# A recurrence on 128-row units: w, k, r channel-major, whole-row scans, matmuls on quarters of the array, fp32 combine

## The chip, the cores and the metric

The kernel runs on one core of a Trainium2 chip. The metric is the device time of one execution in microseconds (us). The engines of the core are named as in the profile: PE (TensorE; its weight loads are PEld), DVE (VectorE), ACT (ScalarE), POOL (GpSimd), and SP, whose queue issues the DMAs.

## The reference

A recurrence with a decaying state per head, and behind it a soft mixture of experts over all tokens. B = 4 batches, H = 8 heads, S = 768 tokens, D = 48 channels; the mixture has 3072 tokens of 384 values, 8 experts with 4 slots each, and 1024 hidden values. All is float32.

```python
state = zeros(B, H, D, D)
for t in range(S):
    cur = einsum('bhd,bhe->bhde', u[None] * kt, vt)
    y[:, :, t] = einsum('bhd,bhde->bhe', rt, state + cur)
    state = wt[:, :, :, None] * state + einsum('bhd,bhe->bhde', kt, vt)
x = y.transpose(0, 2, 1, 3).reshape(B * S, H * D)
logits = x @ phi                                  # 3072 x 32
d = softmax(logits, axis=0);  slot_input = d.T @ x
slot_out[e] = relu(slot_input[e] @ w1[e]) @ w2[e]   # 8 experts x 4 slots
c = softmax(logits, axis=1);  out = c @ slot_out
```

## The kernel before, in words

The work is cut into 16 **pairs**: one batch and two heads (head h on rows 64h to 64h+47 of a 112-row tile). A pair has six **chunks** of 128 tokens. Inside a chunk the decay is taken out by cumulative products: K is divided by the product up to a token and R multiplied by it, so that the chunk becomes a masked score matrix; between chunks a 48x48 state is carried.

For each pair w, k and r come from memory with tokens on the rows (L173). PE transposes w (`a_wT`, L200) and k and r (`a_turn`, L235). DVE makes the backward products G, one scan of 128 per chunk (`a_back`, L212), the forward products Rc from their reciprocals (`a_fwd`, L221), and the scaled KTt and RTt (`a_scale`, L241). PE then turns KTt back (`b_kn`, L279), makes the scores (`b_scores`, L292), the chunk states U (`b_u`, L313) and the two parts of y: masked scores times v (`c_av`, L335) and R times the carried state (`c_inter`, L348). DVE carries the state by a scan per head over U (`b_state`, L321) and adds the diagonal part when it moves y out of PSUM (`c_evac`, L357). That diagonal part is r times k times u, summed: two products on POOL (`d_rk` L254, `d_rku` L260), a sum on DVE (`d_a`, L265), a product with v on POOL (`d_av`, L270). POOL also masks the scores (L297). Then x is transposed (L366) and multiplied with phi (L383), and each batch adds its slot inputs (L428).

The order of each engine's instructions is written out by hand in a loop over 17 steps. A step issues part A (scans and scaling) of one pair, parts B and C (scores, state, y) of the pair before, and the transposes of x for the one before that. Nothing reorders them: an instruction that waits holds back all that stands behind it on its engine. Weights of the experts arrive through the same SP queue during the loop and at its end.

The tail is the experts: `up_proj` (L515), `down_proj` (L549) in two groups of output columns (240 and 144), and `mix` (L593), which combines the slots per token. `mix` splits both factors into a high and a low part in fp32r and contracts 128 rows in one pass; 24 token tiles for each group of columns. The output leaves in 14 stores.

## Time and profile before

| what | value |
|---|---|
| time, median of 3 runs | 245.69 us (244.47 to 246.1) |
| profiled execution, span | 244.0 us |
| PE busy | 211.9 us (87%) |
| DVE busy | 183.7 us (75%) |
| POOL busy | 106.6 us (44%) |
| ACT busy | 97.2 us (40%) |
| mean granted PE clock | 0.946 |
| moved by DMA | 49.54 MB, mean 203 GB/s |

Busy times are shares of the span in which an engine works on an instruction; several engines are busy at once, so they do not add up. The granted clock is the share of PE's full clock that the chip allowed, here in stretches of 3.41 us. The first scan starts at 5.12 us, the first matmul of `up_proj` at 199.93 us; what follows, to the end of the span, is called the tail below.

### The profile page before, as it was taken

The numbers are of one execution on the slowest core, as the hardware profiler recorded it, in microseconds if no ns is written. First come the engines' busy times: TensorE is split into PE (matmuls) and PEld (weight loads), VectorE is DVE, ScalarE is ACT, GpSimd is POOL, SyncE is SP. The second block draws the span as 40 slices with busy tenths as digits, with TensorE's granted clock in tenths as the row PEclk, the third lists the DMA queues.
The fourth block names the chain that finished last, engine by engine and source line by source line (L and its number), as shares of the span: only waits on it lengthen the run. The fifth ranks groups of instructions, "written<-read, shape, count | busy, mean of one in ns | idle before, by whom it ended". The sixth has DMA issues, their size and how long they took to land.

```text
span 244.0 us, 7186 instructions
## 1 busy us (share of the span) xinstructions
PE 211.9 (87%) x2824; PEld 158.8 (65%) x2824; DVE 183.7 (75%) x464; ACT 97.2 (40%) x265; POOL 106.6 (44%) x156
## 2 busy tenths in 40 slices
PE   7759798989898899989798989897989999979850
PEld 3448586868677667768596768687768652346650
DVE  4997969798989888899979798999793744203540
ACT  0623436445262616372544354353536531203330
POOL 5346478465472828382737274563725131000000
PEclk9997979999997999999979999997999999999975
DMA  4988958939795969698696959994959278994994
GB/s 93 181 171 150 178 104 180 199 107 185 223 225 156 230 164 271 119 249 162 207 173 206 179 185 180 309 233 185 288 177 313 68 248 273 318 326 145 334 309 120
DMA packets 122072, 49.54 MB, mean 203 GB/s; under 512 B 101424, under 2 KB 118960, under 8 KB 122032
## 3 DMA queue, kind: packets, MB, share of 16 engines
q1 hardware_dynamic: 122032, 49.02, 79.2%
q8 instruction: 24, 0.39, 0.7%
q14 instruction: 16, 0.13, 0.2%
HBM read 44.29 MB, written 4.72 MB: 201 GB/s over the span
## 4 chain that ended last, share of the span: by engine, by line
PE 44%; DVE 38%; issue 6%; DMA 5%; SPq 2%; ACT 1%; POOL 1%; DVEq 0%; POOLq 0%; ACTq 0%
DVE Rc L221 13%; PE yp L348 13%; DVE G L212 12%; PE yp L335 6%; DVE Sb L321 6%; DVE KTt L241 5%; DMA wt<-in_moe_w_dram 4%; PE wt L200 4%; PE tp L279 4%; PE so L549 3%; PE hp L515 3%; PE op L593 3%; SPq L173 2%; PE sp L428 2%; PE tp L235 2%
## 5 line engine op out<-in xcount | busy, mean ns | idle before, releaser
L270 POOL TENSOR_TENSOR av<-vt,a 128x576 f32<-128x576 f32 x16 | 18.6, 1162 | 60.0 <-DVE x L357 38.9
L235 PE MATMUL tp<-ident,wrk 128*112 128x128 f32 x192 | 32.1, 299 | 13.8 <-DVE KTt L241 13.1
L212 DVE TENSOR_TENSOR_SCAN G<-wt,floor 112x128 f32<-112x128 f32 x96 | 32.0, 401 | 9.9 <-PE wt L200 9.6
L221 DVE TENSOR_TENSOR_SCAN Rc<-wt,Rc,ceil 112x127 f32<-112x127 f32 x96 | 37.6, 459 | 0.6
L348 PE MATMUL yp<-Sb,RTt 112*64 112x96 f32 x320 | 33.7, 353 | 3.8 <-DVE Sb L321 3.3
L235 PEld LDWEIGHTS tp<-ident,wrk 128*112 128x112 f32 x192 | 20.6, 140 | 24.2 <-DVE KTt L241 17.7
L297 POOL TENSOR_SCALAR_AFFINE_SELECT at<-at 128x384 f32<-128x384 f32 x64 | 31.8, 520 | 10.3 <-ACT at L296 10.2
L296 ACT COPY at<-ap 128x384 f32<-128x384 f32 x64 | 27.6, 482 | 20.6 <-PE ap L292 19.8
L281 ACT COPY kn<-tp 128x336 f32<-128x336 f32 (+1 forms) x32 | 11.0, 397 | 56.2 <-PE tp L279 56.2
L335 PEld LDWEIGHTS yp<-vt,at 128*64 128x64 f32 x768 | 29.0, 150 | 3.9 <-issue 1.6
L292 PE MATMUL ap<-RTt,KTt 48*128 48x128 f32 x384 | 30.9, 289 | 0.0
L335 PE MATMUL yp<-vt,at 128*64 128x48 f32 x768 | 30.8, 234 | 0.0
L292 PEld LDWEIGHTS ap<-RTt,KTt 48*128 48x128 f32 x384 | 24.8, 187 | 5.7 <-issue 4.7
L348 PEld LDWEIGHTS yp<-Sb,RTt 112*64 112x64 f32 x320 | 22.3, 157 | 7.2 <-DVE Sb L321 6.1
L254 POOL TENSOR_TENSOR rk<-wrk 128x576 f32<-128x576 f32 x16 | 22.6, 1414 | 9.4 <-ACT rk L205 8.7
L321 DVE TENSOR_TENSOR_SCAN Sb<-up,pat 48x288 f32<-48x288 f32 x32 | 24.0, 749 | 2.1 <-PE up L313 1.9
L260 POOL TENSOR_TENSOR rk<-rk,u_bc 128x576 f32<-128x576 f32 x16 | 22.5, 1405 | 1.9 <-DMA u_bc<-in_u_dram 1.7
L357 DVE TENSOR_TENSOR x<-yp,av 128x288 f32<-128x288 f32 x32 | 14.5, 454 | 7.8 <-PE yp L348 7.7
L241 DVE TENSOR_TENSOR RTt<-tp,Rc 112x384 f32<-112x384 f32 x32 | 16.5, 553 | 2.2 <-PE tp L235 1.8
L241 DVE TENSOR_TENSOR KTt<-tp,G 112x384 f32<-112x384 f32 x32 | 16.0, 538 | 0.0
L200 PE MATMUL wt<-ident,wrk 128*112 128x128 f32 x96 | 14.0, 282 | 1.3 <-POOL rk L254 0.7
L205 ACT ACTIVATE rk<-wrk,b_low 128x576 f32<-128x576 f32 x16 | 12.6, 786 | 6.5 <-DVE a L265 6.5
(125 smaller groups left out, 280.0 us busy)
## 6 DMA issues: line engine op xcount, KB each, us to landing
wt<-in_moe_w_dram SPq DMA_DIRECT2D x24, 512.0 KB, 4.9
wt<-in_moe_w_dram SPq DMA_DIRECT2D x4, 1536.0 KB, 6.9
vt<-in_v_dram SPq DMA_DIRECT2D x16, 288.0 KB, 4.0
wrk<-in_w_dram SPq DMA_DIRECT2D x30, 144.0 KB, 2.9
wrk<-in_k_dram SPq DMA_DIRECT2D x30, 144.0 KB, 3.4
wrk<-in_r_dram SPq DMA_DIRECT2D x30, 144.0 KB, 3.9
wt<-in_moe_w_dram SPq DMA_DIRECT2D x5, 576.0 KB, 8.2
wt<-in_moe_w_dram SPq DMA_DIRECT2D x3, 960.0 KB, 8.5
```

Of the source, the lines that this page charges most:

```text
L200: nc.tensor.transpose(out=wt[0:PITCH, c // 3, (c % 3) * P:(c % 3 + 1) * P], in_=win(st["t"], W_OFF, c), identity=ident)
L212: nc.vector.tensor_tensor_scan(out=G[0:PITCH, c, 0:P][:, ::-1], data0=wc[:, ::-1], data1=floor[0:PITCH].broadcast_to([PITCH, P]), initial= ...
L221: nc.vector.tensor_tensor_scan(out=Rc[0:PITCH, c, 1:P], data0=wc[:, 0:P - 1], data1=ceil[0:PITCH].broadcast_to([PITCH, P - 1]), initial=Rc ...
L235: nc.tensor.transpose(out=tp[0:PITCH, j, :], in_=win(st["t"], off, 3 * hf + j), identity=ident)
L241: nc.vector.tensor_tensor(out=st[which][0:PITCH, cs, :], in0=st[which, hf][0:PITCH], in1=fac[0:PITCH, cs, :], op=ALU.mult)
L254: nc.gpsimd.tensor_tensor(out=rk, in0=chd(st["t"], R_OFF), in1=chd(st["t"], K_OFF), op=ALU.mult)
L292: nc.tensor.matmul(out=aps[h][:, cc, :], lhsT=st["KT"][rows, c, :], rhs=st["RT"][rows, c, :], start=True, stop=True)
L296: nc.scalar.copy(out=at, in_=aps[h])
L297: nc.gpsimd.affine_select(out=at, in_=at, pattern=[[0, 3], [1, P]], compare_op=ALU.is_gt, fill=0.0, base=0, channel_multiplier=-1)
L321: nc.vector.tensor_tensor_scan(out=Sb[rows, h * D:(h + 1) * D, :].rearrange("p e n -> p (e n)"), data0=st["up"][rows].rearrange("p e n -> ...
L335: nc.tensor.matmul(out=yp[cols, cc, h, :], lhsT=st["AT", h, hf][:, cc, cols], rhs=st["vv"][:, h, 3 * hf + cc, :], start=first[th], stop=False)
L348: nc.tensor.matmul(out=st["yp", hf][cols, cc], lhsT=st["RT"][0:PITCH, c, cols], rhs=Sb[0:PITCH, :, c], start=False, stop=(cc == 2))
```

## The change

The host now delivers w, k and r **channel-major** (channels on rows, 768 tokens along a row, with one extra column per chunk: 6 x 129 = 774), and rearranges the output. The rows of a tile are filled: a **unit** has 128 rows, heads 2g and 2g+1 on 48 rows each, and on the 16 rows left over beside each a third of heads 6 and 7. So three units hold a batch's eight heads, and the fourth pair of the batch (heads 6 and 7) is put together from the three scaled units by DMAs from SBUF to SBUF (`a_gather`).

For a unit DVE runs one backward scan over 774 elements (`a_back`, L505; a column of 3e38 restarts it at each chunk), one reciprocal, one product for k in place (`a_k`, L512), one forward scan (`a_fwd`, L515), one product for r in place (`a_r`, L520). No transposes of w, k, r are left on PE. The diagonal part is one product on POOL per unit (`a_rk`, L501, 768 columns), and PE sums it against u into four columns per chunk (`aP`, L572), in the same PSUM bank as U; a DVE copy takes it out (L585). `b_kn` (L535), `b_scores` (L548), `c_inter` (L616) and the transposes of x (`l_turn`, L647) each work on quarters of the array: 64 rows by 64 columns, four places. `b_state` is one scan of 288 for both heads (L588), followed by an ACT copy to a contiguous Tc (L595). All PSUM tiles are fixed; U, aP and the turned k share one bank, y has one buffer for each head.

In the tail there are three groups of columns (160, 160, 64). The slots are gathered onto all four 32-row groups by one matmul (`gather_slots`, L229), and `mix` (L242) is a plain fp32 product of 32 rows, all token tiles of one row group before the next. Output leaves in 5 stores. The later expert weights go into the buffers that the loop frees.

On DVE, one step of the loop for an ordinary pair of **before** (G and Rc are the products of the next pair, Sb the state, x the evacuation):

```order
L304 MEMSET up 128x48
L212 SCALAR_TENSOR_TENSOR G<-wt,floor 112x128 x6
L215 RECIPROCAL Rc<-G 112x6
L221 SCALAR_TENSOR_TENSOR Rc<-wt,Rc,ceil 112x127 x6
L241 TENSOR_TENSOR KTt<-tp,G 112x384 x2
L321 SCALAR_TENSOR_TENSOR Sb<-up,pat_142 48x288 x2
L241 TENSOR_TENSOR RTt<-tp,Rc 112x384 x2
```

There the clearing of U (up) stands ahead of the scans. On DVE in **after**, the third step of a batch and the start of the fourth (blkw holds w, krb k and r of a unit, tp_80 U and aP, Traw the state):

```order
L505 SCALAR_TENSOR_TENSOR G<-blkw,G 128x774
L507 RECIPROCAL blkw<-G 128x6
L512 TENSOR_TENSOR krb_94<-krb_94,G 128x774
L515 SCALAR_TENSOR_TENSOR G<-blkw,G 128x774
L565 MEMSET tp_80 128x48
L588 SCALAR_TENSOR_TENSOR Traw<-tp_80,blkm 112x288
L585 COPY asb_110<-tp_80 128x24
L636 TENSOR_TENSOR x_100<-y_82,av_105 128x6x48
L636 TENSOR_TENSOR x_100<-y_83,av_105 128x6x48
L84 TENSOR_REDUCE nM<-lt 96x1
L520 TENSOR_TENSOR krb_94<-krb_94,G 128x774
```

The clearing of U (L565) has moved behind the scans and products of the step, and the state scan stands right behind it. On PE in **after**, one step from the matmuls that wait for that clearing to the next such place:

```order
L572 MATMUL tp_80<-cst,blka 64x4 x12
L578 MATMUL tp_80<-v_102,blkm 48x48 x10
L548 MATMUL ap_78<-krb_94 64x128 x2
...
L77 MATMUL tp_81<-blkm,cst 32x256 x6
L647 MATMUL ap_78<-cst,x_99 64x64
...
L535 MATMUL tp_80<-cst,krb_93 64x48 x2
...
L616 MATMUL y_82<-Tc_107,krb_94 64x48 x2
...
L627 MATMUL y_82<-v_102,blkat 64x48 x2
...
L572 MATMUL tp_80<-cst,blka 64x4 x12
```

aP (L572) and U (L578) stand behind all of a step's other matmuls except the second half of the scores and the product with phi. On POOL in **after**, the first two steps of a batch (asb is aP copied out, blkat the scores, krb k and r of a unit):

```order
L604 TENSOR_TENSOR av_104<-v_101,asb_110 128x576
L559 AFFINE_SELECT blkat<-blkat 128x384 x2
L501 TENSOR_TENSOR blka<-krb_94 128x768
L523 COPY chk<-krb_94 128x6
L559 AFFINE_SELECT blkat<-blkat 128x384 x2
L602 TENSOR_TENSOR a_112<-a_112,asb_111 128x12
L604 TENSOR_TENSOR av_105<-v_102,asb_111 128x576
```

The product r times k of a unit (L501) stands behind the product with v and two masks, and DVE's in-place product of the same unit (L512) waits for it.

The diff at its core (the kernel is written anew; what is left out is renaming, the setup, and the softmax steps, which are kept):

```diff
...
-COLS = ((0, 240), (240, 384))
...
-    def a_back(i, cs):
-        wt = sts[i]["wt"]
-        for c in cs:
-            wc = wt[0:PITCH, c // 3, (c % 3) * P:(c % 3 + 1) * P]
-            nc.vector.tensor_tensor_scan(
-                out=G[0:PITCH, c, 0:P][:, ::-1], data0=wc[:, ::-1], data1=floor[0:PITCH].broadcast_to([PITCH, P]),
...
-    def a_scale(i, which, hf):
-        st = sts[i]
-        fac = G[:, :, 1:P + 1] if which == "KT" else Rc
-        cs = slice(3 * hf, 3 * hf + 3)
-        nc.vector.tensor_tensor(out=st[which][0:PITCH, cs, :], in0=st[which, hf][0:PITCH],
-                                in1=fac[0:PITCH, cs, :], op=ALU.mult)
...
-        for cc, h in order:
-            c = 3 * hf + cc
-            rows = slice(64 * h, 64 * h + D)
-            nc.tensor.matmul(out=aps[h][:, cc, :], lhsT=st["KT"][rows, c, :], rhs=st["RT"][rows, c, :],
-                             start=True, stop=True)
...
+PIT = P + 1
+ROW = C * PIT
+RO = ROW + 1
+KRW = RO + ROW
...
+COLS = ((0, 160), (160, 320), (320, 384))
...
+    def gather_slots(so, s_sb, rp, S4, wd, act=False):
+        (nc.scalar.copy if act else nc.vector.tensor_copy)(out=s_sb, in_=so)
+        nc.tensor.matmul(out=rp, lhsT=rep, rhs=s_sb, start=True, stop=True)
+        (nc.scalar.copy if act else nc.vector.tensor_copy)(out=S4, in_=rp)
...
+            for r in range(4):
+                op = banks[r][:, 0:per * wd].rearrange("p (i d) -> p i d", d=wd)
+                for i in range(per):
+                    nc.tensor.matmul(out=op[:, i, :], lhsT=cT[32 * r:32 * r + 32, i0 + i, :],
+                                     rhs=S4[32 * r:32 * r + 32, lo:hi], start=True, stop=True)
...
+    U = tp[0][:, 0:D * C].rearrange("p (e n) -> p e n", n=C)
+    aP = tp[0][:, D * C:D * C + 4 * C].rearrange("p (c n) -> p c n", n=4)
...
+    def a_gather(u):
+        s = u % NU
+        for h in range(2):
+            nc.sync.dma_start(out=kr3[64 * h + 16 * s:64 * h + 16 * s + 16, :],
+                              in_=kr4[u % 4][64 * h + D:64 * h + 64, :])
+    def a_rk(u):
+        t = kr4[u % 4]
+        k3 = t[:, 0:ROW].rearrange("p (c e) -> p c e", e=PIT)[:, :, 1:PIT]
+        r3 = t[:, RO:KRW].rearrange("p (c e) -> p c e", e=PIT)[:, :, 0:P]
+        nc.gpsimd.tensor_tensor(out=rks[u % 2], in0=k3, in1=r3, op=ALU.mult)
+    def a_back(u):
+        w = ws[u % 2]
+        nc.vector.tensor_tensor_scan(out=G[:, ::-1], data0=w[:, ::-1], data1=g_one.broadcast_to([P, ROW]),
+                                     initial=1.0, op0=ALU.mult, op1=ALU.min)
+        nc.vector.reciprocal(out=holes(w, 0), in_=holes(Gp, 1))
+    def a_k(u):
+        k = kr4[u % 4][:, 0:ROW]
+        nc.vector.tensor_tensor(out=k, in0=k, in1=Gp[:, 1:ROW + 1], op=ALU.mult)
+    def a_fwd(u):
+        nc.vector.tensor_tensor_scan(out=G, data0=ws[u % 2], data1=g_zero.broadcast_to([P, ROW]),
+                                     initial=1.0, op0=ALU.mult, op1=ALU.add)
+    def a_r(u):
+        r = kr4[u % 4][:, RO:KRW]
+        nc.vector.tensor_tensor(out=r, in0=r, in1=G, op=ALU.mult)
...
+    def b_scores(n, hf):
+        kt, rt = Kt(n), Rt(n)
+        for cc in range(3):
+            c = 3 * hf + cc
+            for h in range(2):
+                for p in range(2):
+                    nc.tensor.matmul(
+                        out=ap[h][64 * p:64 * p + 64, cc * P:(cc + 1) * P],
+                        lhsT=kt[64 * h:64 * h + D, c * PIT + 1 + 64 * p:c * PIT + 65 + 64 * p],
+                        rhs=rt[64 * h:64 * h + D, c * PIT:c * PIT + P], start=True, stop=True)
...
+    def b_u(n):
+        b, g = divmod(n, NG)
+        nc.vector.memset(U[:, :, 0:1], 0.0)
+        kn, vt = kns[n % 2], vts[n % 3]
+        first = [True, True]
+        if g < NU:
+            rk = rks[(NU * b + g) % 2]
+            for c in range(C):
+                for p in range(2):
+                    nc.tensor.matmul(out=aP[64 * p:64 * p + 64, c, :], lhsT=rk[:, c, 64 * p:64 * p + 64],
+                                     rhs=ub[:, g, :], start=first[p], stop=False)
+                    first[p] = False
+        for c in range(C - 1):
+            for h in range(2):
+                rows = slice(64 * h, 64 * h + D)
+                nc.tensor.matmul(out=U[rows, :, c + 1], lhsT=kn[:, h, c, :], rhs=vt[:, c, h, :],
+                                 start=first[h], stop=(c == C - 2))
+                first[h] = False
...
+    def b_state(n):
+        nc.vector.tensor_tensor_scan(
+            out=Traw[0:PITCH].rearrange("p e n -> p (e n)"),
+            data0=U[0:PITCH].rearrange("p e n -> p (e n)"),
+            data1=pats[n % 2][0:PITCH].rearrange("p e n -> p (e n)"),
+            initial=0.0, op0=ALU.add, op1=ALU.mult)
...
+            b_pat(n)
+            u0 = NU * b
+            nxt = b + 1 < B
+            if n == 0:
+                a_rk(1)
+                a_back(1)
+                a_k(1)
+            if j == 0:
+                a_fwd(u0 + 1)
+                a_r(u0 + 1)
+                a_chk(u0 + 1)
+                a_back(u0 + 2)
+            if j == 1:
+                a_k(u0 + 2)
+                a_fwd(u0 + 2)
+                a_r(u0 + 2)
+                a_chk(u0 + 2)
+            if j == 2 and nxt:
+                a_back(u0 + 3)
+                a_k(u0 + 3)
+                a_fwd(u0 + 3)
+            if j == 3 and nxt:
+                a_r(u0 + 3)
+                a_chk(u0 + 3)
+                a_rk(u0 + 4)
+                a_back(u0 + 4)
+                a_k(u0 + 4)
+        lb, lj = divmod(l, NG)
+        if l >= 0 and lj >= 1:
+            l_turn(l)
+        if live:
+            b_kn(n)
+        if m >= 0:
+            c_inter(m)
+        if live:
+            b_scores(n, 0)
+            b_mask(n, 0)
+        if m >= 0:
+            c_av(m)
+        if live:
+            b_u(n)
+            b_state(n)
+            b_a(n)
+            b_av(n)
+        if m >= 0:
+            c_evac(m)
+        if live:
+            b_scores(n, 1)
+            b_tc(n)
+            b_mask(n, 1)
+            if j == 0:
+                a_rk(NU * b + 2)
+            if j == 1 and b + 1 < B:
+                a_rk(NU * b + 3)
...
+    def rows(a):
+        t = a.reshape(B, H, C, P, D).transpose(0, 1, 4, 2, 3)
+        o = np.zeros((B, NU, P, C, P), f)
+        for h in range(2):
+            for g in range(NU):
+                o[:, g, 64 * h:64 * h + D] = t[:, 2 * g + h]
+                o[:, g, 64 * h + D:64 * h + 64] = t[:, 6 + h, 16 * g:16 * g + 16]
+        return o.reshape(B * NU, P, C, P)
```

More of the change, by code (lines that the diff above doesn't have):

```diff
@@ L302, in b_zero @@
-    def b_zero(i):
-        sts[i]["up"] = up = ps_y.tile([P, D, C], F32, name="up", tag="yp")
-        nc.vector.memset(up[:, :, 0:1], 0.0)
-    def b_u(i):
-        st = sts[i]
-        up = st["up"]
-        first = [True, True]
-        for n in range(C - 1):
-            for h in range(2):
-                rows = slice(64 * h, 64 * h + D)
-                nc.tensor.matmul(out=up[rows, :, n + 1], lhsT=st["kn"][:, n, rows], rhs=st["vv"][:, h, n, :],
-                                 start=first[h], stop=(n == C - 2))
-                first[h] = False
@@ L542, in down_proj @@
         lo, hi = cols
+        wd = hi - lo
         fill = list(fill)
@@ new lines, in l_turn @@
+    def l_turn(n, split=False):
+        b, g = divmod(n, NG)
+        kt = g - 1
+        x, xT = xb[b % 2], xTs[kt % 2]
+        for t in range(C):
+            for ch in range(2):
+                for p in range(2):
+                    nc.tensor.matmul(
+                        out=ap[p][64 * ch:64 * ch + 64, t * 64:(t + 1) * 64],
+                        lhsT=x[64 * p:64 * p + 64, t, kt * P + 64 * ch:kt * P + 64 * ch + 64],
+                        rhs=id2[64 * p:64 * p + 64, :], start=True, stop=True)
+        for p in range(2):
+            cp = nc.vector.tensor_copy if split and p else nc.scalar.copy
+            cp(out=xT[:, :, 64 * p:64 * p + 64], in_=ap[p][:, 0:C * 64].rearrange("p (c t) -> p c t", t=64))
@@ new lines, in rwkv_soft_moe, with keep_warm @@
+    zb = const.tile([P, 256], BF16, name="zb")
+    def keep_warm(n, bank):
+        for _ in range(n):
+            nc.tensor.matmul(out=bank[:, 0:256], lhsT=zb[:, 0:P], rhs=zb, start=True, stop=True)
+    a_load_w(0)
+    a_load_kr(0)
+    nc.sync.dma_start(out=cs_t, in_=cst)
+    v_load(0)
+    a_load_w(1)
+    a_load_kr(1)
+    nc.vector.memset(Gp[:, ROW:RO], 1.0)
+    nc.vector.memset(g_one, 1.0)
+    nc.vector.memset(g_zero, 0.0)
+    nc.vector.memset(tp[0], 0.0)
+    nc.vector.memset(zb, 0.0)
@@ L1060, in rwkv_soft_moe @@
[L1060 to L1071 removed]
+    down_proj(hT, so[2], wts, 0, COLS[2], [lambda: fin(1)])
```

1212 lines of the change are left out of this document (484 added, 728 removed).

## The prediction

> **What bounds the kernel now.** I read the page's busy shares and its chain of waits first, then the chain in order of time, then the groups, and last a table of PE's busy time and granted clock in equal stretches.
>
> ```profile
> span 244.0 us, 7186 instructions
> PE 211.9 (87%) x2824; PEld 158.8 (65%) x2824; DVE 183.7 (75%) x464; ACT 97.2 (40%) x265; POOL 106.6 (44%) x156
> PE 44%; DVE 38%; issue 6%; DMA 5%; SPq 2%; ACT 1%; POOL 1%; DVEq 0%; POOLq 0%; ACTq 0%
> ```
>
> PE and DVE share the chain: neither bounds alone, each step hands over from one to the other. The chain in order of time shows where (start, length, what):
>
> ```profile
> 18.23 0.88 PE yp L348 x8
> ...
> 148.82 0.63 PE tp L279 x5
> 149.45 0.67 PE wt L200 x6
> 150.21 2.00 DVE G L212 x6
> 152.47 1.28 DVE Rc L221 x4
> 153.99 0.83 DVE Rc L221 x2
> 154.81 0.91 DVE KTt L241 x2
> 156.40 0.77 DVE Sb L321
> 157.21 0.89 PE yp L348 x8
> 158.10 0.69 PE yp L335 x24
> 158.78 1.03 PE yp L348 x12
> 159.82 0.63 PE tp L279 x5
> ...
> 171.32 0.63 PE tp L279 x5
> ...
> 188.44 0.68 PE yp L348 x8
> ...
> 199.93 2.72 PE hp L515 x24
> ...
> 207.81 9.86 DMA wt<-in_moe_w_dram
> ...
> 223.10 0.64 PE op L593 x4
> ...
> 232.02 3.35 PE op L593 x24
> ```
>
> One step is a loop of 3.9 us on PE, 5.8 on DVE and 1.3 of hand-overs, 11.00 us from one turn of K (L279) to the next (148.82 to 159.82). From the first product with the carried state (L348, 18.23) to that of the last pair (188.44) there are 15 steps: 11.35 us each. The tail from 199.93 to 244.0 takes 44.1 us, with one DMA wait of 9.86 us.
>
> **Part by part: DVE.** The groups give the prices (busy, mean ns of one):
>
> ```profile
> L212 DVE TENSOR_TENSOR_SCAN G<-wt,floor 112x128 f32<-112x128 f32 x96 | 32.0, 401 | 9.9 <-PE wt L200 9.6
> L221 DVE TENSOR_TENSOR_SCAN Rc<-wt,Rc,ceil 112x127 f32<-112x127 f32 x96 | 37.6, 459 | 0.6
> L321 DVE TENSOR_TENSOR_SCAN Sb<-up,pat 48x288 f32<-48x288 f32 x32 | 24.0, 749 | 2.1 <-PE up L313 1.9
> L241 DVE TENSOR_TENSOR KTt<-tp,G 112x384 f32<-112x384 f32 x32 | 16.0, 538 | 0.0
> L357 DVE TENSOR_TENSOR x<-yp,av 128x288 f32<-128x288 f32 x32 | 14.5, 454 | 7.8 <-PE yp L348 7.7
> L265 DVE TENSOR_REDUCE a<-rk 128x12 f32<-128x576 f32 x16 | 11.9, 742 | 0.0
> ```
>
> A scan of 288 takes 750 ns and 96 of 128 take 32.0 us: 2.60 ns per element either way, so 774 elements take 2.02 us. (At the price of L221, 392 ns for 127, it would be 2.39; I take 2.02, since the forward scan has no start value from a tile any more.) A product takes 16.0/32 = 0.50 us for 384 elements, so 1.01 us for 774. A unit is 2.02 + 0.2 (reciprocal) + 1.01 + 2.02 + 1.01 = 6.26 us; three units for four pairs are 4.7 us per step. Before, a step had 2.0 + 2.35 + 2 x 1.0 + 0.2 = 6.55, the sum L265 (0.74) and two state scans (1.5). Those become no sum, one scan (0.75) and a small copy of aP (0.15). DVE loses 3.3 us of work per step.
>
> But the order has changed: U is now cleared behind the scans, the matmuls aP and U wait for that, and the state scan waits for them. Between them DVE does nothing. aP and U are 44 passes, two at a time; L335 has 24 in 0.69 us, or 58 ns for two, so 22 x 58 = 1.28 us, with a hand-over 1.4 (bounds: 1.1 if the narrow passes go faster, 1.8 with slower hand-overs). A step on DVE is then 4.7 + 0.1 (clearing) + 1.4 + 0.75 + 0.15 + 2 x 0.454 + 0.85 (softmax steps, spread over four) = 8.9 us.
>
> **POOL** adds to it.
>
> ```profile
> L270 POOL TENSOR_TENSOR av<-vt,a 128x576 f32<-128x576 f32 x16 | 18.6, 1162 | 60.0 <-DVE x L357 38.9
> L254 POOL TENSOR_TENSOR rk<-wrk 128x576 f32<-128x576 f32 x16 | 22.6, 1414 | 9.4 <-ACT rk L205 8.7
> L297 POOL TENSOR_SCALAR_AFFINE_SELECT at<-at 128x384 f32<-128x384 f32 x64 | 31.8, 520 | 10.3 <-ACT at L296 10.2
> ```
>
> One product of 768 replaces L254 and L260: 1414 x 768/576 = 1.89 us. It lies behind av (1.16) and two masks (0.99) that themselves start at the copy of aP: 4.0 us, after which DVE's in-place product of the same unit may start. In the first step of a batch DVE has only the two evacuations (0.9) meanwhile and waits about 3 us; in the second it reaches the product later and waits about 1.5; else not. That is 4.5 per four steps, 1.1 per step, and with 0.4 of other hand-overs a step is 10.4 us (bounds 9.6 and 11.2 by POOL 20% faster or slower and the two scan prices).
>
> **PE** loses the transposes of w, k, r (L200, L235), and L348 reads a contiguous operand instead of a strided one. By the 58 ns above for a group of passes that run together, with four together on quarters: K turned 40 passes, 0.58; L616 40, 0.58; c_av as before, 2 x 0.69; aP and U 1.3; the transposes of x 48 passes in three of four steps, 0.5; phi 0.45; the scores by the timeline's row (start, length):
>
> ```profile
> 104.44 0.94 PE L292 MATMUL ap<-RTt,KTt 48*128 48x128 f32 x12
> ```
>
> That is half a pair's scores; on quarters there are twice as many passes, twice as many at once, so both halves are 1.9 again. Sum 6.7 us in a step of 10.4: PE is no longer a bound, and waits. DMA brings longer rows and about the same bytes; in the chain it is 5%, nearly all of it the one wait in the tail, so I cost the loads of the loop at nothing; their cover is a step of 10.4 us, and a load that came late would add its own lateness.
>
> **Start and tail.** Two loads before the first scan (5.1 us, as before), then 6.3 for unit 0, 6.3 for unit 1 and 2.0 for unit 2's back scan, b_u 1.4, state 0.8, about 1 for k arriving after w: the first product with the state at 23 instead of 18.2. Then 13 steps of 10.4 and two without scans, bound by PE's 6.7 and its hand-overs, 7.0 each: 23 + 135.2 + 14 = 172.2 instead of 188.4. The next 11.5 us to up_proj are the same work: 183.7. In the tail the combine becomes 24 x 2 passes for each of three groups of columns. A pass of 128 columns takes 0.67/6 = 0.112 us (L200), so one of 160 takes 0.14 and one of 64, by its weight load, 0.058: 6.7 + 6.7 + 2.8 = 16.2 us instead of 24 x 0.16 + 3.35 = 7.2. One group of 6.7 can lie beside the DMA wait, the gathering of slots adds two hand-overs of a us each: between +2.4 and +11, I take +6, the middle. So 183.7 + 44.1 + 6 = 233.8.
>
> **The clock.** PE's granted clock in stretches of 3.41 us (columns: length, then PE, PEld, DVE, ACT, POOL busy, clock, DMA share, GB/s):
>
> ```profile
> 6.01:9.42 3.41, 2.33 (x15) 1.33 (x14) 3.34 (x10) 2.15 (x3) 0.07 (x1) 1.00 0.79 153
> ...
> 70.86:74.27 3.41, 2.18 (x41) 1.76 (x40) 3.34 (x10) 1.91 (x7) 3.41 (x6) 1.00 0.98 314
> 74.27:77.69 3.42, 3.42 (x38) 3.06 (x36) 3.34 (x8) 0.64 (x2) 0.40 (x2) 0.50 0.34 79
> ...
> 118.65:122.06 3.41, 1.62 (x20) 1.15 (x16) 3.37 (x8) 1.61 (x6) 2.01 (x4) 1.00 0.61 245
> 122.06:125.47 3.41, 3.41 (x46) 3.16 (x47) 2.81 (x7) 0.36 (x1) 0.00 (x0) 0.50 0.96 188
> ...
> 214.22:217.63 3.41, 1.70 (x34) 0.81 (x26) 0.00 (x0) 0.00 (x0) 0.00 (x0) 1.00 1.12 325
> 217.63:221.05 3.42, 3.34 (x65) 2.16 (x66) 0.00 (x0) 0.00 (x0) 0.00 (x0) 1.00 1.16 326
> ```
>
> A stretch in which PE was busy 2.18 us or less is followed by one at half clock; after 2.33 it is not. One stretch (1.70, in the DMA wait) speaks against it. In the changed loop PE's mean is 6.7/10.4 x 3.41 = 2.20, and its idle time lies in one piece: from the end of U, PE has 5.4 us of other work while DVE has 7.0 to 8 before the next clearing, and 3 more where POOL holds it. So I expect about one half-clock stretch in each of the 13 full steps, and five more at the start and in the tail: 18. The price of one: the step that holds the one at 166.43 is 171.32 - 159.82 = 11.50 instead of 11.00, so 0.50; if all that PE loses lay on the path, 1.7. The burst that is slowed holds aP and U, which the state waits for, but PE waits again afterwards; I take 0.73, nearer the row. 18 x 0.73 = 13.
>
> Sum: 233.8 + 13 = 246.8 for the profiled execution. That of before is 244.0 where the median is 245.69, 1.7 more; so 248.5.
>
> **Rivals.** First, on the other side: **the clock stays up**, as after the 1.70 stretch, because bursts between waits are dense enough or the wait shorter than worked out. It decides where PE's busy time per stretch stays above 2.2. Then 233.8 + 1.7 = 235.5, faster by 4%; between 230 and 242 by the bounds of a step and the tail. For it: the mean is just at the mark. Against: both stretches with such a wait were followed by half clock. The Trainium skill ("TensorE: Matmul & The Clock Gate", section "Why this matters for your kernels") says that throughput drops after PE-idle gaps above about 3 us, and by that rule few of these waits would count; the rows at 70.86 and 118.65, with 1.2 and 1.8 us idle, disagree with so high a mark, which is why I give this rival less than the forecast.
>
> Second: **quarters run two at a time, not four.** No row shows four. The nearest row is L335, two at a time. Then K turned, L616, scores and the turns of x take twice as long, 3.5 us more per step; PE has 10.2 of 10.4, its wait hides 2, and 1.5 per step stay: 233.8 + 16 x 1.5 + 1.7 = 259, with the clock up. The Trainium skill ("TensorEngine Tiling (Array Packing)", section "Tiling Modes") counts 64x64 as four independent tiles; by it the loop above stands, by the nearest row this rival.
>
> Third: **the combine is not hidden at all**, and the last group's stores follow late: +14 instead of +6 in the tail, 256 with the clock as forecast.
>
> **Chances.** Forecast 0.50 (its own range 242 to 256: a price of 0.50 to 1.0 per stretch, the step's bounds); clock stays up 0.33; quarters two at a time 0.08; combine exposed 0.09. Below 232 lies a tenth (the lower part of the second case), above 258 a tenth: 232 to 258. About 1% (2.5 us) is what a measurement of this kernel can tell from no change. Faster than 243.2: nearly all of the second case and a tenth of the first, 0.38; between 243.2 and 248.2: 0.15; slower: 0.47.
>
> **What would show it.** The clock row of the changed page: half-clock stretches in most steps (forecast), or 9s throughout (first rival). A step of 10.4 us plus clock loss between state scans, with DVE waiting for PE (U) 1.4 us and, twice per batch, for POOL. The matmuls on quarters: groups of four within about 60 ns (scores 112), or two. Scans of 774 at 2.0 us. The tail longer by 6. The forecast is wrong if a step is under 9.5 us, if quarters do not overlap, or if the waits do not lower the clock.

## The result, and the profile after

The changed kernel takes 267.94 us (median; 266.7 to 270.43) where the kernel before takes 245.4: 9.4% longer, ratio 1.094 with a 95% interval of 1.088 to 1.101. Forecast were 248.5 us, between 232 and 258. The sign was that of the likeliest case; the size was not, and the time lies outside the range. From execution to execution the changed kernel and its variants scatter by 0.5 to 7%, the kernel before by about 1%: times below are medians of all executions, good to some 4 us where no interval is given, and ratios with their intervals leave out executions more than 1.5% above the fastest of their kernel, so the two can differ.

The page of the changed kernel (busy shares, granted clock in 40 slices, DMA queues, chain of waits):

```profile
span 265.4 us, 10690 instructions
PE 207.6 (78%) x4804; PEld 165.9 (62%) x4804; DVE 119.6 (45%) x222; ACT 79.2 (30%) x198; POOL 78.7 (30%) x141
PEclk9999998799855558957795795998589789999955
q8 instruction: 39, 0.64, 1.0%
PE 57%; DVE 20%; issue 8%; POOL 6%; ACT 3%; DMA 2%; SPq 1%; ACTq 0%; DVEq 0%; POOLq 0%
```

DVE lost a third of its work, 183.7 to 119.6 us, and is no longer half busy. PE's busy time has hardly changed, with 70% more passes, and 57% of the chain is PE instead of 44%. The clock row has a run of 5s where that of before had single dips.

The chain in order of time, one whole step and what follows (start, length, what):

```profile
53.76 0.76 DVE Traw L588
54.52 0.72 DVE x L636 x2
55.30 0.49 ACT blkat L554
55.84 0.92 PE ap L647 x44
56.76 0.51 PE tp L535 x34
57.33 0.53 PE y L616 x36
57.91 0.67 PE ap L548 x17
58.95 1.40 issue
60.35 1.38 PE y L627 x41
61.73 0.66 PE tp L572 x24
62.39 0.49 PE tp L578 x20
62.88 0.82 PE ap L548 x24
...
67.13 3.65 issue
...
71.57 2.74 PE y L627 x48
74.31 1.21 PE tp L572 x24
75.51 0.87 PE tp L578 x20
```

From the state scan to the last matmul that the next one waits for, all is PE but 2 us of DVE and ACT: turn of x, turn of K, product with the state, scores, masked scores times v, aP, U. DVE's scans are not on it in this step. Twice PE stands still in the middle of a burst with nothing that the profile can name ("issue", 1.40 and 3.65 us). And from 71 us on the same bursts take twice as long: L627 2.74 us instead of about 1.5, aP 1.21 instead of 0.66.

Other steps look different. In the first step of three of the four batches the chain runs over POOL's product and DVE's products and scan, as here behind the state scan at 113.9:

```profile
115.10 1.13 POOL av L604
116.66 0.52 POOL blkat L559
117.17 1.53 POOL blka L501
118.72 0.97 DVE krb L512
119.72 1.79 DVE G L515
121.53 0.96 DVE krb L520
```

In the steps into the third and the fourth batch it runs over DVE's scans. Of the 177 us of the chain in the loop (from 19.5 to 197 us) 99 are PE's, 37 DVE's, 13 POOL's and 15 without a name; the rest are ACT's and the DMA's.

The waits (engine and group, what it waited for: us in all, times, longest) show the same:

```profile
DVE Traw L588 <- PE tp L578: 56.1, 16, 6.2
...
DVE krb L512 <- POOL blka L501: 17.1, 8, 3.9
PE ap L548 <- issue: 7.6, 4, 3.7
PE tp L572 <- DVE tp L565: 6.5, 5, 2.4
PE y L627 <- issue: 1.4, 1, 1.4
PE y L616 <- issue: 1.3, 1, 1.3
```

DVE waits 3.5 us for U on average in each of 16 steps. PE waits for the clearing of U only five times. Where PE's own time goes is in stretches (length, then PE, PEld, DVE, ACT, POOL busy, clock, DMA share, GB/s): two steps from state scan to state scan, and below them a part of the long run at half clock.

```profile
53.76:62.93 9.17, 7.08 (x272) 6.35 (x276) 6.19 (x9) 4.14 (x10) 2.31 (x6) 0.97 0.81 220
62.93:76.44 13.51, 9.86 (x284) 8.55 (x288) 5.36 (x9) 4.23 (x11) 4.97 (x8) 0.81 0.65 219
...
67.96:71.38 3.42, 0.60 (x17) 0.52 (x17) 3.35 (x3) 0.00 (x0) 0.00 (x0) 1.00 0.25 95
71.38:74.79 3.41, 3.41 (x67) 3.29 (x64) 0.20 (x2) 0.86 (x2) 1.18 (x3) 0.50 0.44 61
...
81.62:85.03 3.41, 3.41 (x68) 3.08 (x62) 2.42 (x3) 0.86 (x2) 0.99 (x2) 0.50 0.05 18
85.03:88.44 3.41, 3.41 (x73) 3.32 (x74) 0.42 (x1) 0.00 (x0) 0.00 (x0) 0.50 0.98 338
...
98.68:102.10 3.42, 3.42 (x72) 3.33 (x73) 0.70 (x2) 0.09 (x1) 1.91 (x3) 0.50 0.16 28
102.10:105.51 3.41, 3.41 (x135) 2.21 (x129) 2.00 (x7) 1.44 (x4) 0.99 (x2) 1.00 0.96 348
```

A step at 0.97 of the clock is 9.17 us, one with half clock and the 3.65 us wait 13.51. Once the clock is down here, it stays down for nine stretches, 30.7 us, though in several of them PE is busy from end to end. Before the last stores the granted-clock records hold 85 us at half clock. They begin only at 40.66 us; until then the bursts have the lengths of the half clock (aP 1.45 us at 30.46, where it takes 0.66 at 40.94), so the 9s at the left of the clock row are no full clock. From PE's first work of the loop at 19.5 us that is 21 us more, 106 in all; the kernel before has 17. The half clocks told below are counted in this way.

The state scans start at 21.8, 32.8, 42.1, 53.8, 62.9, 76.4, 88.0, 101.4, 113.9, 127.2, 136.3, 150.0, 162.7, 172.8, 179.5 and 193.6 us; up_proj starts at 210.35 and the span ends at 265.4. By the forecast's own parts: 13 steps take 151.0 us instead of 13 x (10.4 + 0.73) = 144.7; the last two take 20.8 instead of 14; the way from there to up_proj is 16.8 (from the last product with the state, at 196.98, it is 13.4 where 11.5 were forecast); the tail is 55.1 where 44.1 + 6 and 3.6 for the clock were forecast. So 17 of the 19 us that were missed lie before up_proj.

### The profile page after: what moved, and what is told of

Its sections match the earlier page's. It is cut to its first block, busy times and chain, and to the rows that moved or that the text cites. A ratio compares the mean times of both kernels' runs of the same rounds, so it can differ in the third digit from the quotient of the medians.

```text
span 265.4 us, 10690 instructions
## 1 busy us (share of the span) xinstructions
PE 207.6 (78%) x4804; PEld 165.9 (62%) x4804; DVE 119.6 (45%) x222; ACT 79.2 (30%) x198; POOL 78.7 (30%) x141
## 4 chain that ended last, share of the span: by engine, by line
PE 57%; DVE 20%; issue 8%; POOL 6%; ACT 3%; DMA 2%; SPq 1%; ACTq 0%; DVEq 0%; POOLq 0%
PE y L627 9%; PE ap L548 8%; DVE G L515 5%; PE G L186 5%; PE tp L572 4%; PE tp L578 4%; PE y L222 4%; PE ap L647 4%; PE y L616 3%; PE tp L535 3%; PE tp L242 3%; POOL blka L501 3%; DVE G L505 3%; PE ap L242 3%; DVE krb L520 3%
## 5 line engine op out<-in xcount | busy, mean ns | idle before, releaser
L554 ACT COPY blkat<-ap 128x384 f32<-128x384 f32 x64 | 27.7, 481 | 106.8 <-PE ap L548 106.8
L559 POOL TENSOR_SCALAR_AFFINE_SELECT blkat<-blkat 128x384 f32<-128x384 f32 x64 | 31.9, 521 | 37.7 <-ACT blkat L554 37.7
L627 PE MATMUL y<-v,blkat 128*64 128x48 f32 x768 | 36.1, 269 | 1.7 <-issue 1.4
L588 DVE TENSOR_TENSOR_SCAN Traw<-tp,blkm 112x288 f32<-112x288 f32 x16 | 12.1, 756 | 56.1 <-PE tp L578 56.1
L627 PEld LDWEIGHTS y<-v,blkat 128*64 128x64 f32 x768 | 33.7, 184 | 5.5 <-issue 4.9
L548 PE MATMUL ap<-krb 48*64 48x128 f32 x576 | 30.6, 345 | 8.2 <-issue 5.3
L548 PEld LDWEIGHTS ap<-krb 48*64 48x64 f32 x576 | 22.5, 173 | 8.6 <-issue 3.9
L572 PE MATMUL tp<-cst,blka 128*64 128x4 f32 x288 | 14.0, 225 | 12.9 <-DVE tp L565 6.5
L505 DVE TENSOR_TENSOR_SCAN G<-blkw,G 128x774 f32<-128x774 f32 x12 | 21.3, 1771 | 2.5 <-DMA blkw<-in_wc_dram 2.3
L572 PEld LDWEIGHTS tp<-cst,blka 128*64 128x64 f32 x288 | 13.3, 184 | 13.9 <-DVE tp L565 7.1
L515 DVE TENSOR_TENSOR_SCAN G<-blkw,G 128x774 f32<-128x774 f32 x12 | 21.3, 1772 | 0.3
L501 POOL TENSOR_TENSOR blka<-krb 128x768 f32<-128x768 f32 x12 | 18.6, 1552 | 4.0 <-DMA krb<-in_krc_dram 4.0
L512 DVE TENSOR_TENSOR krb<-krb,G 128x774 f32<-128x774 f32 x12 | 11.5, 958 | 17.1 <-POOL blka L501 17.1
L647 PEld LDWEIGHTS ap<-cst,x 64*64 64x64 f32 x576 | 13.3, 174 | 7.1 <-ACT blkat L554 4.4
L535 PE MATMUL tp<-cst,krb 48*64 48x48 f32 x480 | 13.0, 252 | 4.9 <-DVE krb L512 4.0
L535 PEld LDWEIGHTS tp<-cst,krb 48*64 48x64 f32 x480 | 11.8, 168 | 7.8 <-DVE krb L512 4.5
L647 PE MATMUL ap<-cst,x 64*64 64x64 f32 x576 | 15.5, 266 | 1.4 <-ACT blkat L554 1.2
L616 PE MATMUL y<-Tc,krb 48*64 48x48 f32 x480 | 13.8, 269 | 2.2 <-issue 1.3
L578 PE MATMUL tp<-v,blkm 128*48 128x48 f32 x320 | 14.4, 259 | 0.0
L616 PEld LDWEIGHTS y<-Tc,krb 48*64 48x64 f32 x480 | 12.5, 186 | 2.6 <-issue 1.5
L604 POOL TENSOR_TENSOR av<-v,asb 128x576 f32<-128x576 f32 x12 | 14.1, 1175 | 0.0
```

The source lines that it names most:

```text
L501: nc.gpsimd.tensor_tensor(out=rks[u % 2], in0=k3, in1=r3, op=ALU.mult)
L505: nc.vector.tensor_tensor_scan(out=G[:, ::-1], data0=w[:, ::-1], data1=g_one.broadcast_to([P, ROW]), initial=1.0, op0=ALU.mult, op1=ALU.min)
L515: nc.vector.tensor_tensor_scan(out=G, data0=ws[u % 2], data1=g_zero.broadcast_to([P, ROW]), initial=1.0, op0=ALU.mult, op1=ALU.add)
L535: nc.tensor.matmul(out=tp[h][64 * p:64 * p + 64, c * D:(c + 1) * D], lhsT=kt[64 * h:64 * h + D, c * PIT + 1 + 64 * p:c * PIT + 65 + 64 * p ...
L548: nc.tensor.matmul(out=ap[h][64 * p:64 * p + 64, cc * P:(cc + 1) * P], lhsT=kt[64 * h:64 * h + D, c * PIT + 1 + 64 * p:c * PIT + 65 + 64 * p],
L554: nc.scalar.copy(out=at.rearrange("p c t -> p (c t)"), in_=ap[h][:, 0:384])
```

## The experiments

Theories. **A**: as forecast, DVE's order and POOL's product set the step, and the idle stretch of PE lowers the clock. **B**: PE itself sets the step, by its matmuls, its waits for instructions and its clock, and what DVE does lies beside it. Beside both, what the loads in the loop and the combine cost was open.

**Fillers on PE.** Ahead of aP, where the forecast had PE idle for 2 to 3.5 us:

```diff
+        if 1 <= n < NIT:
+            for _ in range(3):
+                nc.tensor.matmul(out=ap[0], lhsT=ident, rhs=cs_t[:, 0:512], start=True, stop=True)
         if live:
             b_u(n)
```

> Three fp32 matmuls of 512 columns (2.6 us at full clock) whose result nobody reads are put on PE ahead of aP in every step from the second on, where it waits. Theory A (the half clock costs what the forecast missed): half-clock time falls from 85 us to under 40, aP and U take 1.1 us in most steps instead of 2.1, and the time falls by 8 to 15, to 253 to 260. Theory B (the half clock lies beside waits anyway): clock up, time within 3 of 268. Theory C: PE is itself late in many steps, then the filler lies on the path: 275 to 290.

Measured 289.5 us, ratio 1.178 (1.174 to 1.181), 21.6 more than the changed kernel. The half clock before the last stores fell from 106 to 61 us, so these matmuls of 512 columns do hold the clock up. But of the 15 x 2.6 = 39 us of filler more than half ended on the path. PE has no idle 2.6 us there: theory C of the expectation, B here.

**Clearing U earlier**, in the middle of the scans:

```diff
             if j == 0:
                 a_fwd(u0 + 1)
                 a_r(u0 + 1)
                 a_chk(u0 + 1)
+                b_zero()
                 a_back(u0 + 2)
```

> Theory A (the order on DVE is what costs most: U is cleared behind the scans, so that PE stands still for 2 to 6 us in a step, DVE for 1.4 us and more, and the idle stretch lowers the clock): with the clearing moved into the middle of the scans, PE works on aP and U while DVE scans, a step falls from 11.5 us to 8 to 9, half-clock time falls from 85 us before the last store to under 40, and the time from 268 to 225 to 240. Theory B (late loads behind the gathers and waits of PE for its own instructions set the step): a step stays above 10.5, the time 255 to 265.

Measured 306.1 us, ratio 1.246 (1.241 to 1.252): neither. The turn of K writes the same bank as U, and stood behind the clearing in the program, so it now waited for it:

```profile
DVE Traw L590 <- PE tp L580: 106.4, 16, 8.7
...
PE tp L535 <- DVE tp L564: 46.3, 12, 6.2
```

46 us of PE's waits went to the turn of K, which had waited for no clearing before. The second try moves the turn of K (and of x) ahead of the scans in the program, which changes no engine's order but makes the clearing wait for it:

```diff
         if live:
             b_pat(n)
+        if l >= 0 and lj >= 1:
+            l_turn(l)
+        if live:
+            b_kn(n)
             u0 = NU * b
...
```

> As the first try at clearing U in the middle of the scans, but the turn of K stands ahead of the scans in the program, so that it does not wait for the clearing (the two share a bank), but the clearing for it. Theory A (the order on DVE costs most): PE works on aP and U while DVE scans; a step falls from 11.5 us to 8 to 9.5 and the time from 268 to 235 to 250. Theory B (clock, instruction waits and loads set the step): a step above 10.8, the time 258 to 268.

Measured 261.9 us (256.7 to 265.5), about 6 less: theory B of the expectation. PE no longer waits for the clearing, and a step is still 10.9 us on average (11.45 in the changed kernel). The order on DVE was worth some 6, with no interval, not 20 to 30.

**POOL's product of r and k first.**

```diff
             b_a(n)
+            if j == 0:
+                a_rk(NU * b + 2)
             b_av(n)
...
-            if j == 0:
-                a_rk(NU * b + 2)
```

> In the first step of a batch POOL's product of r and k stands ahead of the product with v and the masks, not behind them. Theory A (DVE's wait of 3.2 to 3.9 us there is on the path, four times): DVE's wait for it falls from 17 us to under 6, the time by 6 to 14, to 254 to 262. Theory B (PE at half clock is late there anyway): the wait goes, the time falls by less than 3.

Measured 267.7 us, ratio 1.082 (1.075 to 1.089): no change by the medians, some 3 us less by the ratio. The wait itself went:

```profile
DVE krb L512 <- POOL blka L501: 4.5, 5, 1.5
```

from 17.1 to 4.5 us, and the time stayed or nearly so: theory B of the expectation. POOL and DVE had been on the path in those steps, but PE's own loop is nearly as long there. In the chain of the loop POOL falls from 13 to 3 us and DVE from 37 to 21, and PE rises from 99 to 133; the first steps of the batches fell from 11.0, 13.5, 13.3 and 10.1 us to 10.5, 10.9, 12.4 and 8.8, the second of which had held the 3.65 us wait. The profiled execution has 136 us of half clock instead of 106, which is part of PE's rise.

**The loads' order on SP.** Loads of the next units and of v ahead of the gather:

```diff
         if j == 1 and live:
             a_gather(NU * b)
-        if j in (1, 2) and live:
-            a_gather(NU * b + j)
         if j >= 1 and u_next < B * NU and live:
             a_load_w(u_next)
             a_load_kr(u_next)
         if n + 1 < NIT:
             v_load(n + 1)
+        if j in (1, 2) and live:
+            a_gather(NU * b + j)
```

> On SP's queue the loads of the next units and of v stand ahead of the gathers that wait for DVE, not behind them. Theory A (the queue's order made k and r of a unit come 5 us late): the wait of POOL's product for the DMA at 125 us goes, and with it the half-clock stretches around it: 5 to 8 us less, 260 to 263. Theory B (the load takes long because the DMA is shared, not because it starts late): within 2 of 268.

Measured 268.2 us, ratio 1.093 (1.087 to 1.098): no change. But not for theory B's reason. The wait for k and r at 125 us (4.93 us in the chain of the changed kernel) is gone from the chain; elsewhere in the loop there are other stretches that the chain puts to "issue":

```profile
60.52 2.30 issue
82.31 2.34 issue
127.21 2.82 issue
150.48 5.71 issue
```

The longest of them, 5.71 us, lies between two of POOL's instructions, and behind it the chain has a new wait of 3.73 us for the DMA of the weights. Of PE's own waits without a name the list of waits has 11.0 us, against 10.3. The wait for k and r was not won back as time: the step in which it had ended is 11.4 us now, and was 9.1. That the earlier loads stand in the way elsewhere is a guess that no run tests.

**Weights left out of the loop.** 21 of the 27 pieces are not loaded, and all experts read the same first weights:

```diff
-    pieces = iter([(n, a) for n in range(N_WA) for a in range(KT)])
+    pieces = iter([(n, a) for n in (2, 7) for a in range(KT)])
...
-    wts = wa[0:E] + [t[:, 0:WF] for t in [wa[E],
+    wts = [wa[2]] * E + [t[:, 0:WF] for t in [wa[7],
```

> Leaves out 21 of the 27 pieces of expert weights that are loaded in the loop (all experts read the same first weights), so 11 MB less go through the DMA engines there. Theory A (the waits of PE within a burst, 1.3 to 3.7 us each at five places, come from its own instructions, fetched through the same DMA engines, standing behind data): those waits shrink to under 0.5 us and the time falls by 5 to 12. Theory B (they come from the scheduling of the burst itself): they stay, and the time stays within 3 of 268.

Measured 254.9 us, ratio 1.039 (1.028 to 1.050): 13 less by the medians (of two executions here), 11 between the profiled executions, 9 of these ahead of the last state scan. The waits of PE that have no name:

```profile
PE ap L548 <- issue: 3.5, 3, 1.5
...
PE y L627 <- issue: 1.7, 1, 1.7
```

PE's unnamed waits fall from 10.3 to 5.2 us, with the same 39 fetches of instructions, and the wait of 4.93 us for k and r is gone from the chain. The half clock hardly changes (98 us). So 11 MB of weights, which no engine waits for by name in the loop of the changed kernel, cost some 11 to 13 us, at the upper end of theory A; the waits shrank, but not to under 0.5 us each. The step that had held the wait of 3.65 us fell from 13.5 to 10.1 us. What the late unit cost is not separated: the step in which its wait ended was one of the shortest, 9.1 us.

**Half as many matmuls.** Two tests of the number of instructions. First the four groups on quarters back to row halves, 128 columns of weights at a time, here for the turn of K:

```diff
-                for p in range(2):
-                    nc.tensor.matmul(
-                        out=tp[h][64 * p:64 * p + 64, c * D:(c + 1) * D],
-                        lhsT=kt[64 * h:64 * h + D, c * PIT + 1 + 64 * p:c * PIT + 65 + 64 * p],
-                        rhs=id2[64 * h:64 * h + D, 0:D], start=True, stop=True)
+                nc.tensor.matmul(
+                    out=tp[h][:, c * D:(c + 1) * D], lhsT=kt[64 * h:64 * h + D, c * PIT + 1:c * PIT + 1 + P],
+                    rhs=id2[64 * h:64 * h + D, 0:D], start=True, stop=True)
...
```

> Undoes the quarters: the turn of K, the scores, the product with the state and the turns of x work on two row halves with 128 columns of weights, half as many matmuls, each moving as many columns as before; all else as in the changed kernel. Theory A (quarters double the instructions, and PE waits for its instructions): the waits of 1.3 to 3.7 us within bursts fall from 10 us to under 4 and the time by 5 to 12, to 256 to 263. Theory B (what counts is the weight load: 128 columns take longer than 64): bursts of the turn of K and of the state take 1.5 times as long, and the time rises by 3 to 10. Theory C: they cancel, within 3 of 268.

Measured 316.1 us, ratio 1.275 (1.260 to 1.289), 48 more by the medians, 44 by the ratios. Then only the scores on halves, and aP and the masked scores times v with whole-array weights:

```diff
-                for p in range(2):
-                    nc.tensor.matmul(
-                        out=yb[h][64 * p:64 * p + 64, c * D:(c + 1) * D],
-                        lhsT=ats[n % 2][h][c // 3][:, c % 3, 64 * p:64 * p + 64],
+                nc.tensor.matmul(
+                    out=yb[h][:, c * D:(c + 1) * D], lhsT=ats[n % 2][h][c // 3][:, c % 3, :],
...
```

> Scores on row halves, aP and masked scores times v with all 128 columns of weights: half as many matmuls in these three, by the rows each group as long as before (scores move 128 columns either way; aP and c_av are one load of 128 columns instead of two of 64). A fifth fewer instructions on PE; the turn of K, the product with the state and the turns of x stay on quarters. Theory A (PE waits for its instructions): the waits within bursts fall from 10 us to under 5, the time by 4 to 10, to 258 to 264. Theory B (the data of the loads alone cause the waits): within 3 of 268. Theory C (a load of 128 columns costs twice one of 64 in these groups too, as with the turn of K on halves): 275 to 290.

Measured 318.0 us (306.4 to 324.8). Both times the unnamed waits all but vanish (none listed, and 0.8 us; 29 and 32 fetches instead of 39), and both times it is far slower. The vanishing does not tell why the waits were there: the first try at clearing U, at 306 us, lists 0.3 us of them with all 39 fetches. The timeline of PE, the first of the two kernels, then the second, then the changed kernel (start, length, passes), all at half clock, the second by the lengths of its bursts, since its clock records begin later:

```profile
111.11 2.32 PE L534 MATMUL tp<-cst,blka 48*128 48x48 f32 x20
113.23 2.34 PE L612 MATMUL y<-Tc,krb 48*128 48x48 f32 x20
```

```profile
29.70 5.35 PE L623 MATMUL y<-v,blkat 128*128 128x48 f32 x24
```

```profile
94.19 1.26 PE L535 MATMUL tp<-cst,blka 48*64 48x48 f32 x40
```

On quarters the same turn takes 1.26 us for 40 passes, and L627 2.74 for 48. Each pass moves 48 columns in all of these, and with 128 columns of weights instead of 64 a burst takes nearly twice as long with half as many passes: here the columns of the weights set the time. The half clock rose to 210 us in the first, so part of its time is clock. The quarters are worth 44 to 48 us to this kernel, the clock included; what the unnamed waits cost can't be read from these runs, since PE's bursts grew around them.

The same two on top of other edits say the same: 285.4 (276.4 to 293.5) and 301.2 us (292.5 to 308.7).

> The same on top of the combination of the clearing amid the scans, the product of r and k first, and the combine over row groups. Theory A: 5 to 12 under the combination's 254, so 242 to 249. Theory B: 257 to 264.

> Both of these on top of the combination (clearing amid the scans, product of r and k first, combine over row groups). If they add to its 254: 240 to 247, about the kernel before. If fewer matmuls cost weight loads: 258 to 275.

**The softmax steps.** PE's transposes of a batch's exponentials wait, in order, for DVE's maximum and ACT's exponential; the step to a batch's last pair took 13.4 to 14.1 us.

```diff
+        if j == 2 and 0 <= b - 1 < B - 1:
+            qs[b - 1] = s_max(b - 1, lts[b - 1])
+            s_exp(b - 1, qs[b - 1])
         u_next = NU * (b + 1) + j - 1
...
         if j == 2 and 0 <= sb_ < B - 1:
-            qs[sb_] = q = s_max(sb_, lts[sb_])
-            s_exp(sb_, q)
+            q = qs[sb_]
             s_dturn(q, dpv)
```

> The maximum and the exponential of a batch's slot softmax are issued at the start of the third step, ahead of its scans, not at its end; PE's transposes of them stay where they are. Theory A (PE, in order, waits for them, and the step to a batch's last pair is 13.4 to 14 us for that): those three steps fall to 11 to 12, the time by 4 to 7. Theory B (half clock makes those steps long): within 2 of 268.

Measured 262.6 us, ratio 1.059 (1.055 to 1.062): 5.4 less by the medians, some 9 by the ratios. The time is theory A's, the steps are not: they went from 13.4 to 12.7, from 13.7 to 12.2 and from 14.1 to 13.9, 2.4 us in all, and none reached 11 to 12. The largest gain, 3.4 us, is in the step that had held the unnamed wait of 3.65 us. So it is not shown that these hand-overs cost 5 us.

**The combine over row groups.**

```diff
-            for r in range(4):
-                op = banks[r][:, 0:per * wd].rearrange("p (i d) -> p i d", d=wd)
-                for i in range(per):
+            for i in range(per):
+                for r in range(4):
+                    op = banks[r][:, 0:per * wd].rearrange("p (i d) -> p i d", d=wd)
                     nc.tensor.matmul(out=op[:, i, :], lhsT=cT[32 * r:32 * r + 32, i0 + i, :],
```

> The combine's matmuls go over the four 32-row groups innermost, token tiles outside. Theory A (in one row group a pass waits for its own weight load, 85 to 125 ns a pass): four groups at once take 24 passes in about 0.9 us instead of 2.0 and the last 48 in 1 us instead of 6: 6 to 9 us less, 259 to 262. Theory B (the copies out of PSUM and the stores behind them bound the tail): 1 to 3 less.

Measured 259.8 us, ratio 1.054 (1.047 to 1.060): 8.1 less, theory A. The last 48 passes, in the chain of the changed kernel and then of this one:

```profile
249.81 2.16 PE ap L242 x21
...
252.31 3.50 PE tp L242 x21
```

```profile
244.45 0.33 PE ap L242 x2
...
246.32 0.19 PE ap L242 x2
```

6.0 us become 2.1. Within one row group a pass of 64 columns takes 0.103 us at full clock (21 in 2.16) and 0.167 us at the half clock that begins at 252.3 us (21 in 3.50); with the row groups innermost four take 0.11 us at full clock. The Trainium skill ("TensorE: Matmul & The Clock Gate", section "The mechanism") says that a weight load overlaps matmuls in flight only where the row group differs; these two runs agree.

**Sums.** Clearing, POOL's product and the combine together:

> U cleared amid the scans with the turn of K ahead of them, the product of r and k first on POOL, and the combine over the row groups innermost. If the three parts lie at different places and add up: 268 minus 8 (the combine, measured) minus 6 to 14 minus 18 to 33: 215 to 235, faster than before. If clock and instruction waits take back what is gained: 240 to 252.

254.0 us (244.8 to 257.1), no interval. With the softmax edit as well:

> The clearing amid the scans, the product of r and k first, the combine over row groups and the early softmax maximum together, all on quarters. If each keeps what it gave alone (6, 0, 8 and 5): 249. If the half clock takes back part: 252 to 256.

250.4 us, ratio 1.019 (1.010 to 1.028): the single gains of 6, 0, 8 and 5 by the medians add up to within 2 us. And with the turn of K ahead of the turns of x:

```diff
             b_pat(n)
+            b_kn(n)
         if l >= 0 and lj >= 1:
             l_turn(l)
         if live:
-            b_kn(n)
```

> As the sum, and the turn of K stands ahead of the turns of x on PE, so that the turns of x, which share a bank with the second half of the scores, come after ACT has copied these. Theory A (PE's 0.6 us of waiting in each of 11 steps is on the path): 4 to 6 under the sum. Theory B (the scores that follow then wait for the copies of the turned x instead): within 2 of the sum.

254.0 us (244.9 to 257.6): nothing that can be told. Two last runs on the sum: four bf16 matmuls of 512 columns ahead of each turn of x, and, in a second kernel without these, the weights left out as above.

```diff
         if l >= 0 and lj >= 1:
+            for _ in range(4):
+                nc.tensor.matmul(out=tp[1], lhsT=zb[:, 0:P], rhs=cs_t[:, 0:256].bitcast(BF16), start=True, stop=True)
             l_turn(l)
```

> The sum of the four edits, and four bf16 matmuls of 512 columns (0.85 us at full clock, nobody reads them) ahead of each turn of x, where PE waits 0.6 us for ACT. They take no more than the wait, but the array streams all through them. Theory A (the half clock costs 0.6 us for each 3.4 us of it): half-clock time before the last store falls by 30 us or more and the time by 4 to 8, to 242 to 246. Theory B (the half clock lies beside other waits): the clock rises, the time stays at 250 or rises by the part of 0.2 us in 11 steps.

> The sum of the four edits without 21 of the 27 pieces of weights loaded in the loop (all experts read the same first weights). Theory A (their cost is a cause of its own): again 10 to 14 less, 237 to 240. Theory B (they hurt through the same path as the others): 3 to 7 less.

The first gave 247.9 us, ratio 1.011 (1.006 to 1.015), about 2.5 less than the sum (medians; by the two profiled executions 7). Its half clock is 62 us, the sum's 94. So 32 us less of it, bought with some 2 us of work where PE had waited 0.6 each time, gave 2.5 to 7: between the two theories, and in keeping with the line fitted below. The second gave 241.9 us as the median of twelve executions from 230.1 to 247.0, 8.5 less than the sum and between its two expectations; its ratio of 0.944 (0.938 to 0.949) rests on the two fastest, 231 us, and puts it 18 less, past both. Either is more than theory B's 3 to 7: the loads cost something of their own beside what the other edits won back, but how much is not settled. PE's unnamed waits fall with them, from 16.7 us in the sum to 7.6. No version that does the whole work is shown to be faster than the kernel before.

## Why the prediction was right or wrong

- **"PE is no longer a bound, and waits": this step failed.** PE was summed to 6.7 us of a 10.4 us step set by DVE and POOL. In the trace a step at 0.97 of the clock is 9.17 us with PE busy 7.08, and the chain through it is PE; over the loop PE has 99 of the chain's 177 us. The fillers show that PE has no 2.6 us to spare; taking 13 us of waits off DVE, in steps where POOL and DVE were on the chain, gained 3 us at most, since PE's loop is about as long there. PE's 7.1 is near the 6.7; what was left out is that PE's bursts form a loop by themselves (the state needs U, the turn of x needs the evacuation and ACT's copies out of the same bank), and that 1.4 to 3.7 us of standing still come on top in some steps. Theory B holds in this form: PE's loop is the longer one or stands close behind.
- **"I cost the loads of the loop at nothing": this failed by some 11 to 13 us**, the largest unpriced term. Their cover was taken to be the length of a step; what shrank without them is less a wait for data than PE's standing still within bursts, which the page shows only as "issue". The kernel before has no such wait in its list of PE's waits; the changed one issues 4804 passes instead of 2824, and its instruction queue 39 fetches instead of 24.
- **The softmax steps at 0.85 us per step, on DVE alone**: issuing two of them earlier gave 5 us or more, of which the three steps in question show 2.4; where the rest came from is open. The last batch's two final steps took 20.8 us instead of 14, which no run takes apart.
- **DVE's prices held**: scans 1.77 us (forecast 2.02), products 0.96 (1.01), state 0.76 (0.75). So did POOL's product, 1.55 (1.89). They lie beside PE, or where they are on the chain PE's loop is close behind, and so were worth little.
- **The step of 10.4 came out for the wrong reason.** A straight line through 78 steps of six profiled executions (the changed kernel, the edits on loads, POOL, softmax and combine) gives 10.2 us for a step without half clock and 0.17 us more for each us of half clock (standard error 0.03), 0.59 for a stretch (forecast 0.73); it explains a quarter of the scatter between steps. But by the chain this is for the most part PE's length with its standing still, not DVE's, so that it is near 10.4 is luck.
- **The clock: price nearly right, number and rule wrong.** 31 stretches (106 us) instead of 18, the first six of them before 40 us, then runs of up to nine. At 0.59 that is 18 us instead of 13. In the 13 full steps the line gives 147.3 us, 2.6 more than forecast; the other 3.7 of the 6.3 us by which they were too long lie outside it. The forecast read the mark from PE's busy time, 2.2 us of 3.41; the stretches at 81.62, 85.03 and 98.68 are busy throughout, and only the last of these three is followed by full clock. The rival that the clock stays up is refuted.
- **Quarters four at a time: right.** 34 passes of the turn of K take 0.51 us, 60 ns for four; the rival of two at a time is refuted, and the runs on halves put the worth of the quarters at 44 to 48 us.
- **The combine: +6, measured 8.1 that can be had back.** The last group's passes were priced too low, 0.058 instead of 0.103 us at full clock and 0.167 at half. The tail as a whole came out near the forecast, 55.1 against 53.7 us.
- **POOL's chain, +1.1 per step: on the path in the first steps of three batches, but worth little**: the run with the product first gained 3 us at most, where 13 steps at 1.1 make 14.

What stays open: by which path the loads cost what they cost, what the unnamed waits are, and what a full clock throughout would give, since no run had one.

## What to carry to other kernels

When an engine is relieved, look whether the other half of the chain can run any faster: here DVE lost 64 us of work, the chain moved to PE for the most part, and the time grew. Here matmuls that move 48 to 64 columns took their time by the columns of their weights, so cut the columns of the weights and put different row groups next to each other; and look for an engine's waits that the profile can't name, which came with 70% more passes here. An instruction that shares a PSUM bank with another can't be moved past it in the program without turning the wait around.

## What the runs showed of the hardware

- The granted clock does not follow PE's busy time here. Stretches at half clock in which PE was busy for all of 3.41 us, with short passes (PEld 3.1 to 3.3 us), were followed by half clock again; matmuls of 512 columns among them cut the half clock from 106 to 61 us, and weight loads of twice the columns raised it to 210, in a loop 45 us longer. That it is the streaming that counts is an inference from these three. The Trainium skill ("TensorE: Matmul & The Clock Gate", section "What's actually happening") puts the half clock down to at least one idle window of about 3.4 us. The long run began in keeping with that, behind a stretch in which PE was busy 0.60 of 3.42 us; but the full stretches in it have no idle time and kept the half clock, so here idle windows alone don't explain it.
- This kernel is faster without loads that no instruction waits for, and PE stands still less in mid-burst: with 11 MB less in the loop these waits fell from 10.3 to 5.2 us, and on the sum from 16.7 to 7.6, one profiled execution each; with loads issued earlier they stayed (11.0). That PE waits for instructions fetched through the same DMA engines would fit the fetches (39 against 24 before), but it is not shown: the waits are gone (0.3 us) in the first try at clearing U too, with its 39 fetches, and in the wait of 3.65 us the DMA engines were busy only 0.46 of the time.
- Weights of 128 columns cost nearly twice what those of 64 do in fp32 passes of 48 columns: at half clock 20 passes on row halves took 2.32 us, 40 on quarters 1.26.
